# First batch of an attention and MLP kernel: sums of q and k by accumulating matmuls, sums of v and most lower parts of x on GpSimd

## The chip, the cores and the metric

The kernel runs on one core of a Trainium2 chip. The metric is the device time of one execution in microseconds. The engines are named as in the profile: PE (TensorE, with its weight loads as PEld), DVE (VectorE), ACT (ScalarE), POOL (GpSimd) and SP (SyncE, which here only issues DMAs).

## The reference

Attention with two branches, and an MLP on its result. q, k and v have the shape 8 x 8 x 576 x 64 (batch, heads, tokens, head size).

```python
q_d = q.reshape(B, H, Sd, 4, D).mean(axis=3)      # and k_d, v_d: means of four tokens
out_up = np.repeat(softmax(scale * q_d @ k_d.T) @ v_d, 4, axis=2)
mask = np.abs(pos[:, None] - pos[None, :]) < 4    # each token and three neighbours on either side
out_local = softmax(where(mask, scale * q @ k.T, -1e9)) @ v
x = (out_up + out_local).transpose(0, 2, 1, 3).reshape(4608, 512)
h = x @ w_in                                      # 512 x 2048
out = (np.maximum(h, 0) + alpha * np.minimum(h, 0)) @ w_out
```

w_in and w_out are 64-bit floats; everything else is fp32.

## The kernel before

**The MLP** is the long part. Its 4608 rows are cut into 18 chunks of 256 rows, and its 2048 hidden columns into 8 pairs of 128, which makes 144 steps. A step runs `hidden` (L761, PE: 24 matmuls), `slopes` (L772 to L776, ACT), `larger` (L782, POOL, in the first 12 steps, L784, DVE, later), `split` (L789, ACT and L71, POOL) and `product` (L818, PE: 12 matmuls). Each operand is held as two fp32r numbers, an upper part (the number rounded) and a lower part (what the rounding left), and three products of the parts make one product. x is held so in `xT[chunk]`, tiles xh and xl.

**The weights** arrive as 64-bit floats and are turned into fp32 by integer operations: `make` (L165) issues for each 1 MB block `magnitude` (L188, ACT), `reach` (L192, L193, DVE), `bits` (L197, L198, DVE), `upper` (L203 or L207, ACT) and `lower` (L211 or L215, DVE). The blocks are loaded into three slots in turn (`load_raw`, L134; L149 for w_in, L153 for w_out), so a load waits until `bits` has read the block three turns earlier. Five of the eight pairs are decoded ahead of the steps.

**Attention** of batches 1 to 7 is spread over the steps: `down` (L228) for the branch of means, `local` (L573) for the neighbours. `down` loads q, k and v of two heads in six loads into three buffers (L236) and folds four tokens into one on POOL (`fold`, L239; the adds appear as L74, the line of the helper `add`). Its `flip` (L254, PE) transposes the sums of q and k; as the tiles of these sums have one buffer each, the folds of the next pair of heads wait for it. The first pair of batch 1 comes before the steps.

**Attention of batch 0** is done first, by `first_batch`, whose generator `pair(hp)` handles heads 2hp and 2hp+1. Its loads are 72 partitions of 8 tokens: qk[hp] for q and k (L400), vt[hp] for v (L403), and windows of v (L412 to L416). PE transposes q and k (L432), ACT copies them out (L436, L440), and PE makes scores of 9 windows of 64 tokens against 70 keys (L448, L452). For the branch of means DVE adds in two halvings over q and over k (L460, in place, and L462), PE transposes the sums into the PSUM tile `fsum` (L467), ACT copies them out scaled (L470, L473) and PE makes the scores `sd` (L476). DVE adds over v likewise (L478, L480). Softmax runs on DVE and ACT (L330 to L338 for the means, L488 to L495 for the windows), PE transposes the probabilities (L344, L500) and multiplies by v (L508, L516), DVE joins the two branches (L519), ACT writes the upper part (L525) and DVE the lower part (L526). For w0 = 0 and 4 these are the chunks 0 and 1 of x; the last 64 tokens stay in `rest`. Pair 3 is the last of the four, and `hidden` of the first steps needs x of all four pairs.

**Order.** DVE, ACT, POOL and SP each run their instructions in one queue. Up to planned time 14 (in steps) that order is not written down: the framework orders the instructions of the program by a simulated timeline when it builds the kernel (`schedule_with_timeline_sim`), under the dependencies between tiles. Events from 14 on keep the order of their planned times. The batch-0 code, the decode of five pairs of weight blocks and the first 15 steps all lie in the first part. The DMAs of the start are issued by SP in the order of the string `ORDER` and then as their buffers are planned.

Of the kernel before, what the change touches and what calls it, by code (L numbers as in the profile page):

```python
# [9 lines left out]
F32 = mybir.dt.float32  # L10
# [3 lines left out]
ALU = mybir.AluOpType  # L14
# [4 lines left out]
FACTOR = 4  # L19
# [33 lines left out]
def tile_attention_moe(ctx: ExitStack, tc: tile.TileContext, q, k, v, w_in, w_out, alpha, out):  # L53
    nc = tc.nc
# [9 lines left out]
    def bank(kind, name):  # L64
        return ps_a.tile([128, 512], F32, tag=f"p{kind}", name=name, bufs=2 if kind == "d" else 1)

    def f32(ap):
        return ap.bitcast(F32)

    def sub(o, a, b):  # L70
        nc.gpsimd.tensor_tensor(o, a, b, op=ALU.subtract)  # L71

    def add(o, a, b):
        nc.gpsimd.tensor_tensor(o, a, b, op=ALU.add)  # L74
# [5 lines left out]
    ident = const.tile([128, 128], F32, name="ident")  # L80
# [274 lines left out]
    def operand(c):  # L355
        if c not in xT:
            pool = late if c % 3 == 2 else two
            xT[c] = [pool.tile([128, 4, T], F32R, tag=f"x{x}", name=f"x{x}{c}") for x in "hl"]
        return xT[c]
# [10 lines left out]
    def first_batch(st):  # L370
# [23 lines left out]
        qk, vt, vw = {}, {}, {}  # L394
# [24 lines left out]
        def pair_bank(kind, name):  # L419
            if kind == "o":  # L420
                return ps_o.tile([128, 512], F32, tag="po", name=name)
            if kind == "h":
                return ps_h.tile([128, 512], F32, tag="ph", name=name)
            return bank(kind, name)

        def pair(hp):
            halves = [slice(64 * e, 64 * e + 64) for e in range(2)]
            for x in range(2):
                for t0, nt in ((0, 4), (4, 4)):
                    ps = ps_h.tile([128, 512], F32, tag="ph", name=f"f{x}T{hp}{t0}")[:, 0:72 * nt]  # L430
# [12 lines left out]
            for part in ("sd", "ds")[EM[hp] == "b"]:  # L443
                if part == "s":
                    banks = []
                    for w0, nw in ((0, 7), (7, 2)):
                        ps = bank("q" if w0 == 0 else "l", f"fs{hp}{w0}")
                        nc.tensor.matmul(ps[:, 0:KEYS * nw], unit,  # L448
                                         wmask[:, w0:w0 + nw].rearrange("p w j -> p (w j)"), start=True, stop=False)
                        for i in range(nw):  # L450
                            w = w0 + i
                            nc.tensor.matmul(ps[:, KEYS * i:KEYS * i + KEYS], qb[:, w].rearrange("p e i -> p (e i)"),  # L452
                                             kT[:, WIN * w:WIN * w + KEYS], start=False, stop=(i == nw - 1))
                        banks.append((w0, w0 + nw, ps[:, 0:KEYS * nw].rearrange("p (w j) -> p w j", j=KEYS)))
                else:
                    sums = []
                    for i, x in enumerate("qk"):
                        lv = qk[hp][:, i].rearrange("p (g f) h d -> p g (f h d)", g=2)
                        s4 = lv[:, :, 0:256]
                        nc.vector.tensor_tensor(s4, lv[:, :, 0:256], lv[:, :, 256:512], op=ALU.add)  # L460
                        s2 = st.tile([72, 2, 128], F32, tag=f"fs2{x}", name=f"fs2{x}{hp}")
                        nc.vector.tensor_tensor(s2, s4[:, :, 0:128], s4[:, :, 128:256], op=ALU.add)  # L462
                        sums.append(s2)
                    ps = ps_h.tile([128, 512], F32, tag="ph", name=f"fsum{hp}")
                    for x in range(2):
                        for g in range(2):
                            nc.tensor.transpose(ps[:, (2 * x + g) * 72:(2 * x + g) * 72 + 72], sums[x][:, g],  # L467
                                                ident[:72, :72])
                    for e, r in enumerate(halves):
                        nc.scalar.mul(qd[r, :, 48 * e:48 * e + 48].rearrange("p b (i g) -> p b i g", g=2),  # L470
                                      ps[r, 0:144].rearrange("p (g b i) -> p b i g", g=2, b=3), DSCALE)
                    kd = st.tile([128, 144], F32, tag="fkh", name=f"fkd{hp}")
                    nc.scalar.copy(kd, ps[:, 144:288])  # L473
                    sd = bank("d", f"fsd{hp}")[:96, 0:432].rearrange("p (b c) -> p b c", b=3)
                    for bl in range(3):
                        nc.tensor.matmul(sd[:, bl, :], qd[:, bl, :], kd, start=True, stop=True)  # L476
            lv = vt[hp].rearrange("p h (g f) d -> p (h g) (f d)", g=2)
            nc.vector.tensor_tensor(lv[:, :, 0:128], lv[:, :, 0:128], lv[:, :, 128:256], op=ALU.add)  # L478
            vd = st.tile([72, 2, 2, 64], F32, tag="fs2v", name=f"fvd{hp}")
            nc.vector.tensor_tensor(vd.rearrange("p h g d -> p (h g) d"), lv[:, :, 0:64], lv[:, :, 64:128], op=ALU.add)  # L480
            if EM[hp] == "b":
                th = yield from down_probs(0, hp, sd)
            mx = one.tile([128, NWIN], F32, tag="lmx", name=f"fmx{hp}")
# [2 lines left out]
            p = st.tile([128, NWIN, KEYS], F32, tag="p", name=f"fp{hp}", bufs=2)  # L486
            for a_, b_, s in banks:
                nc.vector.tensor_reduce(out=mx[:, a_:b_], in_=s, axis=AX.X, op=ALU.max)  # L488
                nc.vector.tensor_tensor(p[:, a_:b_], s, mx[:, a_:b_].unsqueeze(2).to_broadcast([128, b_ - a_, KEYS]),
                                        op=ALU.subtract)  # L490
# [6 lines left out]
            for w0, nw in ((0, 4), (4, 4), (8, 1)):  # L497
                ps = pair_bank(FPT[hp][w0 // 4], f"fpt{hp}{w0}")
# [6 lines left out]
            for g in range(2):  # L505
                for e, r in enumerate(halves):
                    pr = th[g].rearrange("p (b e a) -> p b e a", b=3, e=2)[:, :, e]
                    nc.tensor.matmul(po[r, 0:144].rearrange("p (b a) -> p b a", b=3), vd[:, e, g], pr,  # L508
                                     start=(g == 0), stop=(g == 1))
            odf = st.tile([128, SD], F32, tag="odf", name=f"fod{hp}")  # L510
            nc.scalar.copy(odf, po[:, 0:144])
            for w0, nw in ((0, 4), (4, 4), (8, 1)):
                ps = pair_bank(FPV[hp][w0 // 4], f"fpv{hp}{w0}")
                for i in range(nw):
                    for e, r in enumerate(halves):
                        nc.tensor.matmul(ps[r, WIN * i:WIN * i + WIN], vw[hp][:, w0 + i, e, :],  # L516
                                         pT[:, w0 + i, 64 * e:64 * e + 64], start=True, stop=True)
                xs = rest[:, hp, :] if w0 == 8 else st.tile([128, 256], F32, tag="xs", name=f"fxs{hp}{w0}")
                nc.vector.tensor_tensor(  # L519
                    xs.rearrange("p (a r) -> p a r", r=4),  # L520
                    ps[:, 0:WIN * nw].rearrange("p (a r) -> p a r", r=4),
                    odf[:, 16 * w0:16 * (w0 + nw)].unsqueeze(2).to_broadcast([128, 16 * nw, 4]), op=ALU.add)
                if w0 < 8:
                    hi, lo = (t[:, hp, :] for t in operand(w0 // 4))
                    nc.scalar.copy(hi, xs)  # L525
                    nc.vector.tensor_tensor(lo, xs, f32(hi), op=ALU.subtract)  # L526
            yield

        return load_pair, load_windows, pair
# [322 lines left out]
    with tc.tile_pool(name="start", bufs=1) as start:  # L852
        load_pair, load_windows, pair = first_batch(start)
        todo = [(w, fp) for fp in range(NP) for w in range(2)]
        for step in ORDER.split():
            kind, i = step[0], int(step[1])
# [45 lines left out]
    for p in range(4 * (B - 1)):  # L902
        b, hp = 1 + p // 4, p % 4
# [92 lines left out]
```

## Time and profile before

| | |
|---|---|
| times of three runs | 998.66, 1002.87, 1002.91 us; median 1002.87 |
| span of the profiled execution | 999.3 us (its time around the span is not listed) |
| mean granted TensorE clock | 0.974 |
| busy, share of the span: PE | 954.3 us, 95% |
| DVE | 826.9 us, 83% |
| ACT | 558.1 us, 56% |
| POOL | 511.7 us, 51% |
| steady stream of `hidden` and `product` begins | 99.4 us |

A chain of work is followed back from the last instruction, at each step to what released it. In the timeline and in the groups of instructions, a name before the arrow is the tile written and the names behind it are those read; "x4" counts instructions that are put together in one row, and the bracket at the end gives the idle time of the engine before the row with what ended it.

### The profile page before, as it was taken

What the parts mean: (1) busy time and instruction counts of PE and PEld (TensorE: products, weight loads), DVE (VectorE), ACT (ScalarE), POOL (GpSimd) and SP (SyncE); (2) the same over time, 40 slices, a digit from 0 to 9 for tenths busy, and PEclk for the clock granted to TensorE, in tenths of its full rate; (3) what the DMA queues carried; (4) which work ended last, traced back from release to release, by engine and by line L of the source; (5) the groups of instructions that cost most, each with busy time, mean ns of one, the idle gap of its engine ahead of it and who ended that gap; (6) DMA issues with size and microseconds to landing.
All of it is one profiled execution on the core that took longest, in us unless ns stands there. A gap on an engine that the chain in (4) does not pass through costs nothing.

```text
span 999.3 us, 17971 instructions
## 1 busy us (share of the span) xinstructions
PE 954.3 (95%) x6402; PEld 851.0 (85%) x6402; DVE 826.9 (83%) x1336; ACT 558.1 (56%) x1483; POOL 511.7 (51%) x624
## 2 busy tenths in 40 slices
PE   5866999799999999999999999999999999999998
PEld 4745988698889988888988888898889888999897
DVE  6998888879898889988889888899898889997111
ACT  4856876355655564655565555565556564544442
POOL 2174867557576546655547355555456632324221
PEclk9956899899999999999999999999999999999999
DMA  8945723233423322332322423323333312210000
GB/s 193 231 162 181 253 88 101 71 107 92 128 86 91 121 71 90 115 100 77 121 73 88 123 86 83 115 85 87 114 91 113 98 55 68 80 33 22 1 22 22
DMA packets 63197, 98.28 MB, mean 98 GB/s; under 512 B 23556, under 2 KB 28932, under 8 KB 63108
## 3 DMA queue, kind: packets, MB, share of 16 engines
q1 hardware_dynamic: 62916, 96.88, 33.0%
q8 instruction: 50, 0.82, 0.4%
q10 hardware_dynamic: 192, 0.26, 0.1%
q14 instruction: 39, 0.32, 0.1%
HBM read 87.67 MB, written 9.44 MB: 97 GB/s over the span
## 4 chain that ended last, share of the span: by engine, by line
PE 87%; DVE 6%; DMA 3%; SPq 2%; ACT 1%; issue 1%; POOL 0%; ACTq 0%; DVEq 0%; POOLq 0%
PE h L761 40%; PE o L818 39%; PE s L267 2%; PE pv L301 2%; DMA raw<-in_moe_w_in 2%; PE xp L666 1%; PE pT L291 1%; SPq L400 1%; PE qkT L254 1%; DVE qk L598 1%; DMA raw<-in_moe_w_out 1%; DVE temp L197 1%; DMA ld<-in_k 0%; DVE temp L198 0%; DVE ls L602 0%
## 5 line engine op out<-in xcount | busy, mean ns | idle before, releaser
L71 POOL TENSOR_TENSOR gl<-t,gh 128x512 fp32r<-128x512 f32 x144 | 186.3, 1293 | 353.1 <-ACT gh L789 340.8
L772 ACT ACTIVATE t<-h,slope 128x256 f32<-128x256 f32 x288 | 136.5, 474 | 160.1 <-PE h L761 128.5
L761 PE MATMUL h<-xh,wih 128*128 128x256 f32 x1152 | 191.5, 287 | 13.3 <-ACT sh L774 6.9
L818 PE MATMUL o<-woh,gh 128*128 128x512 f32 x576 | 194.1, 408 | 0.0
L818 PE MATMUL o<-wol,gh 128*128 128x512 f32 x576 | 187.4, 396 | 0.0
L818 PE MATMUL o<-woh,gl 128*128 128x512 f32 x576 | 187.3, 396 | 0.0
L761 PEld LDWEIGHTS h<-xh,wih 128*128 128x128 f32 x1152 | 165.1, 191 | 24.4 <-ACT sh L774 7.1
L761 PE MATMUL h<-xh,wil 128*128 128x256 f32 x1152 | 185.7, 283 | 0.0
L761 PE MATMUL h<-xl,wih 128*128 128x256 f32 x1152 | 185.1, 282 | 0.0
L784 DVE TENSOR_TENSOR t<-h,t 128x512 f32<-128x512 f32 x132 | 90.6, 686 | 107.5 <-ACT h L776 105.8
L74 POOL TENSOR_TENSOR ld<-ld 72x256 f32<-72x256 f32 x168 | 136.1, 812 | 54.1 <-DMA ld<-in_q 48.8
L761 PEld LDWEIGHTS h<-xh,wil 128*128 128x128 f32 x1152 | 158.7, 191 | 0.4
L761 PEld LDWEIGHTS h<-xl,wih 128*128 128x128 f32 x1152 | 158.0, 190 | 0.5 <-POOL xl L71 0.2
L789 ACT CAST gh<-t 128x512 fp32r<-128x512 f32 x144 | 89.3, 620 | 121.1 <-DVE t L784 82.8
L602 DVE TENSOR_REDUCE ls<-qk 128x12 f32<-128x768 f32 (+1 forms) x126 | 136.2, 1083 | 2.9
L818 PEld LDWEIGHTS o<-woh,gl 128*128 128x128 f32 x576 | 108.1, 188 | 26.0
L818 PEld LDWEIGHTS o<-wol,gh 128*128 128x128 f32 x576 | 107.9, 188 | 24.7
L657 DVE TENSOR_TENSOR lb<-lb,pv 128x384 f32<-128x384 f32 x202 | 113.9, 564 | 5.6
L776 ACT ACTIVATE h<-h,sign 128x256 f32<-128x256 f32 x264 | 116.0, 439 | 0.0
L818 PEld LDWEIGHTS o<-woh,gh 128*128 128x128 f32 x576 | 99.2, 189 | 16.8 <-issue 3.0
L654 DVE TENSOR_TENSOR pv<-v,lb 128x1152 f32<-128x1152 f32 x84 | 93.6, 1115 | 2.6
L598 DVE TENSOR_TENSOR qk<-k,qp 128x768 f32<-128x768 f32 (+1 forms) x78 | 83.8, 1076 | 0.0
(151 smaller groups left out, 1136.7 us busy)
## 6 DMA issues: line engine op xcount, KB each, us to landing
k<-in_k SPq DMA_DIRECT2D x41, 384.0 KB
v<-in_v SPq DMA_DIRECT2D x41, 384.0 KB
out<-sg SPq DMA_DIRECT2D x140, 64.0 KB
raw<-in_moe_w_in SPq DMA_DIRECT2D x16, 512.0 KB
raw<-in_moe_w_out SPq DMA_DIRECT2D x16, 512.0 KB
ld<-in_q SPq DMA_DIRECT2D x56, 144.0 KB
ld<-in_k SPq DMA_DIRECT2D x56, 144.0 KB
ld<-in_v SPq DMA_DIRECT2D x56, 144.0 KB
```

The source lines that it names most:

```text
L71: nc.gpsimd.tensor_tensor(o, a, b, op=ALU.subtract)
L74: nc.gpsimd.tensor_tensor(o, a, b, op=ALU.add)
L598: nc.vector.tensor_tensor(st["pr"][:, :nd], window(tiles[u, "k"], half, d0, nd), st["qp", half].unsqueeze(1).to_broadcast([128, nd, 2, 192 ...
L602: nc.vector.tensor_reduce(out=st["s"][:, half, d0:d0 + nd, :].rearrange("p a b -> p (a b)"), in_=st["pr"][:, :nd].rearrange("p a h (t d) - ...
L654: nc.vector.tensor_tensor(st["pr"][:, :nd], window4(tiles[u, "v"], half, d0, nd), prob(half, d0, nd), op=ALU.mult)
L657: nc.vector.tensor_tensor(st["acc"], st["acc"], st["pr"][:, i], op=ALU.add)
L761: nc.tensor.matmul(ph[:, j], w[:, m, 128 * o:128 * o + 128], x[:, m, :], start=(i == 0), stop=(i == 11))
L772: nc.scalar.activation(t[:, j], hs[st][:, j], AF.Copy, scale=slope[:, f:f + 1])
L776: nc.scalar.activation(other[:, j], hs[st][:, j], AF.Copy, scale=sign[:, f:f + 1])
L784: nc.vector.tensor_tensor(gs[st], hs.pop(st), gs[st], op=ALU.max)
L789: nc.scalar.copy(gh, t)
L818: nc.tensor.matmul(outs[c][m], g[:, j, 128 * m:128 * m + 128], wo[w][n][:, o, :], start=(f == 0 and i == 0), stop=(f == NF - 1 and i == 2))
```

## The change

It touches only `pair` in `first_batch`, in three places.

1. The sums of four tokens of q and k no longer run on DVE. For each of the four parts of `fsum` PE issues four matmuls against the identity, one for each token, which accumulate in PSUM; so 16 matmuls per pair of heads take the place of four transposes, and the four DVE adds per pair (L460, L462) with their two tiles of sums are gone. qk[hp] is no longer overwritten.
2. The two sums of v per pair (L478, L480) move from DVE to POOL.
3. The lower part of x (L526) moves from DVE to POOL, but for the first chunk of pair 3.

```diff
-                    sums = []
-                    for i, x in enumerate("qk"):
-                        lv = qk[hp][:, i].rearrange("p (g f) h d -> p g (f h d)", g=2)
-                        s4 = lv[:, :, 0:256]
-                        nc.vector.tensor_tensor(s4, lv[:, :, 0:256], lv[:, :, 256:512], op=ALU.add)
-                        s2 = st.tile([72, 2, 128], F32, tag=f"fs2{x}", name=f"fs2{x}{hp}")
-                        nc.vector.tensor_tensor(s2, s4[:, :, 0:128], s4[:, :, 128:256], op=ALU.add)
-                        sums.append(s2)
                     ps = ps_h.tile([128, 512], F32, tag="ph", name=f"fsum{hp}")
                     for x in range(2):
                         for g in range(2):
-                            nc.tensor.transpose(ps[:, (2 * x + g) * 72:(2 * x + g) * 72 + 72], sums[x][:, g],
-                                                ident[:72, :72])
+                            for f in range(FACTOR):
+                                nc.tensor.matmul(ps[:, (2 * x + g) * 72:(2 * x + g) * 72 + 72],
+                                                 qk[hp][:, x, FACTOR * g + f].rearrange("p h d -> p (h d)"),
+                                                 ident[:72, :72], start=(f == 0), stop=(f == FACTOR - 1))
...
-            nc.vector.tensor_tensor(lv[:, :, 0:128], lv[:, :, 0:128], lv[:, :, 128:256], op=ALU.add)
+            add(lv[:, :, 0:128], lv[:, :, 0:128], lv[:, :, 128:256])
             vd = st.tile([72, 2, 2, 64], F32, tag="fs2v", name=f"fvd{hp}")
-            nc.vector.tensor_tensor(vd.rearrange("p h g d -> p (h g) d"), lv[:, :, 0:64], lv[:, :, 64:128], op=ALU.add)
+            add(vd.rearrange("p h g d -> p (h g) d"), lv[:, :, 0:64], lv[:, :, 64:128])
...
-                    nc.vector.tensor_tensor(lo, xs, f32(hi), op=ALU.subtract)
+                    if hp == 3 and w0 == 0:
+                        nc.vector.tensor_tensor(lo, xs, f32(hi), op=ALU.subtract)
+                    else:
+                        sub(lo, xs, f32(hi))
```

`add` and `sub` are the helpers of L73 and L70, which issue the operation on POOL.

## The prediction

> **What bounds the kernel now.** I read the chain that ended last first, then asked for busy times by stage, with the stages cut where the chain changes its engine.
>
> ```profile
> 0.00:44.70 44.70, 30.39 (x215) 26.49 (x215) 34.36 (x74) 26.65 (x68) 5.64 (x26) 1.00 0.96 212
> 44.70:73.80 29.10, 18.08 (x155) 13.42 (x156) 29.10 (x49) 18.79 (x48) 23.50 (x15) 0.66 0.54 176
> 73.80:99.40 25.60, 16.39 (x118) 13.71 (x118) 22.28 (x32) 16.47 (x42) 11.37 (x10) 0.63 0.54 171
> 99.40:180.00 80.60, 80.60 (x528) 72.46 (x529) 71.79 (x104) 57.52 (x149) 59.44 (x68) 0.96 0.44 141
> ...
> 196.40:999.30 802.90, 798.24 (x5324) 716.35 (x5324) 653.79 (x1061) 431.69 (x1162) 404.20 (x497) 1.00 0.28 83
> ```
>
> The columns are the stage, its length, the busy time of PE, PEld, DVE, ACT and POOL with their instructions, the granted clock, the DMA share and GB/s. Up to 44.7 us the DMA engines are 96% busy and bound the stage. From 44.7 to 73.8 us DVE is busy for all 29.10 us: it is the bound there, and POOL beside it is 81% busy. From 99.4 us PE is busy without a gap, and after 196.4 us for 798.24 of 802.90 us. A change to the first batch can therefore act on little but how early PE's steady stream starts.
>
> The chain of work says the same in order of time (start, length, what):
>
> ```profile
> 40.50 4.19 DMA raw<-in_moe_w_in
> 44.69 0.17 DVE fp L489
> ...
> 73.76 1.93 PE fpt L500 x8
> ...
> 81.36 0.54 POOL s2q L74
> ...
> 92.20 3.92 DMA raw<-in_moe_w_in
> ...
> 99.37 5.49 PE h L761 x24
> ```
>
> DMA holds the chain until 44.69, DVE until pair 3's probabilities are normalised (L495, 73.7). Then PE transposes them, runs on to the flip of batch 1's first pair, POOL folds the next pair behind it, SP gets to the next weight load only behind the loads into the folded buffers, ACT takes that weight ahead of the activations of `slopes`, and then `hidden` goes on.
>
> **The change part by part.** *Taken from DVE in the DVE-bound stretch.* The shares of the chain between 44.7 and 73.8 by line, and the removed pieces that this line does not list:
>
> ```profile
> by line: DVE temp L197 17.4%; DVE temp L198 12.5%; DVE wil L211 7.6%; DVE xl L526 6.7%; DVE temp L193 6.3%; DVE temp L192 6.2%; DVE wol L215 5.2%; DVE fp L495 5.0%; DVE fsm L492 5.0%; DVE fqk L460 3.9%; DVE dnb L330 3.5%; DVE fxs L519 3.4%;
> ...
> 46.45 0.34 DVE fs2q L462
> ...
> 49.67 0.87 DVE fs2k L462
> ...
> 51.26 0.10 DVE fvd L480
> ...
> 68.50 0.32 DVE fvd L480
> ```
>
> Of 29.1 us, xl's 6.7% are 1.95 and fqk's 3.9% are 1.14. With 0.34 + 0.87 + 0.10 + 0.32 that makes 1.95 + 1.14 + 1.63 = **4.7 us** of a chain that stays on DVE throughout. What is late next in this stretch is again DVE (mostly the decode of the weights, L192 to L215), so I count the removal in full. Its ends are 0, if that decode then waits for weights, and 4.7.
>
> *Taken from DVE before 44.7.* Between 20 and 44.7 us DVE's instructions on the tiles fqk (L460, L462) and fv (L478, L480) are, in this order:
>
> ```profile
> 20.00:44.70 24.70, 5.00 (x9) 1.00 1.03 228
> ...
> 20.00:44.70 24.70, 1.78 (x3) 1.00 1.03 228
> ```
>
> That is 6.8 us. The DMA share of 1.03 hides most of it: weights that have not arrived cannot be decoded earlier. At worst it is worth 0, at best 6.8 plus the wait for v below. I value it by the lag of one operation that had its input:
>
> ```profile
> 34.22 0.74 ACT L491 ACTIVATE fp<-fp 128x630 f32<-128x630 f32 x1
> ...
> 35.24 0.69 DVE L478 TENSOR_TENSOR fv<-fv 72x512 f32<-72x512 f32 x1 [2.03 <-DMA fv<-in_v]
> ...
> 36.91 0.80 DVE L492 TENSOR_REDUCE fsm<-fp 128x9 f32<-128x630 f32 x1
> ```
>
> Pair 1's exponentials end at 34.96, and their sum starts 1.95 us later, because DVE stood 2.03 us at the head of its queue for v's data and then ran sums that now go away. The wait moves to POOL. I take **2.0 us**, with 0 and 6.8 + 2.0 = 8.8 as ends; it is the lower part, since DMA is the bound of that stage.
>
> *Added to POOL.* Eight additions for v and seven subtractions. These are the nearest rows, and what happens when both engines work at once:
>
> ```profile
> L71 POOL TENSOR_TENSOR gl<-t,gh 128x512 fp32r<-128x512 f32 x144 | 186.3, 1293 | 353.1 <-ACT gh L789 340.8
> ...
> 46.39 3.87 POOL L74 TENSOR_TENSOR ld<-ld 72x256 f32<-72x256 f32 x2 [39.82 <-DMA ld<-in_q]
> ...
> 51.09 2.83 POOL L74 TENSOR_TENSOR ld<-ld 72x256 f32<-72x256 f32 x1
> ...
> 65.47 0.72 POOL L74 TENSOR_TENSOR ld<-ld 72x256 f32<-72x256 f32 x1
> ...
> 40.66 0.41 DVE L526 TENSOR_TENSOR xl<-fxs,xh 128x256 fp32r<-128x256 f32 x1
> ...
> 64.53 0.67 DVE L526 TENSOR_TENSOR xl<-fxs,xh 128x256 fp32r<-128x256 f32 x1
> ```
>
> A subtraction of 128x256 has half of gl's elements, so an estimate of 0.65 us; beside a busy DVE it can take up to four times that, as the same fold took 0.72 and 2.83 us. The first sum of v has 72x512 outputs, twice the fold, so 1.4 us, and the second 0.7: 8.5 us in all for four pairs. POOL is idle for 39.82 us up to 46.39, which covers the v sums; what is queued behind them are batch 1's folds, whose data come only then. Without that cover they would push those folds back by as much. The four subtractions that DVE makes between 44.9 and 73.8 come to 2.6 to 10 us of POOL, just before a time in which POOL waits:
>
> ```profile
> POOL s2q L74 <- PE qkT L254: 9.8, 1, 9.8
> ...
> SPq L236 <- POOL s2k L74: 10.7, 4, 4.9
> ```
>
> So those folds end later, but inside the 9.8 us for all but the upper end. The price that I do count is on DVE: an operation beside POOL's took 0.67 instead of 0.41 us, 0.26 more, and four times that is **1.0 us**. The ends are 0 (POOL's work falls beside other reads) and four times 0.54, 2.2 us, by the sum of q or k:
>
> ```profile
> 35.85 0.68 DVE L460 TENSOR_TENSOR fqk<-fqk 72x512 f32<-72x512 f32 x1
> ...
> 46.70 1.22 DVE L460 TENSOR_TENSOR fqk<-fqk 72x512 f32<-72x512 f32 x1
> ```
>
> The Trainium skill, SBUF — State Buffer, section "SBUF: two separate sides", speaks against this part: VectorE, in instructions with two SBUF inputs among others, and GpSimd take a shared port pair as an exclusive lock for a whole instruction, and whichever comes second blocks fully. By that rule a subtraction on GpSimd could hold VectorE up for longer than the subtraction it is rid of, and the four would lose about 1 us (4 x 0.65 against 4 x 0.41) where the sum here gains 0.9 by them (1.95 less 1.0). The trace agrees that such pairs slow each other (0.67 against 0.41), not that all of it is lost.
>
> *Added to PE.* Per pair 16 accumulating matmuls take the place of 4 transposes, 48 more in all. Matmuls of about the same number of columns:
>
> ```profile
> 26.27 4.11 PE L452 MATMUL fs<-kT,qb 128*128 128x70 f32 x18 [0.90 <-ACT kT L440]
> ...
> 50.37 2.12 PE L452 MATMUL fs<-kT,qb 128*128 128x70 f32 x18
> ```
>
> That is 0.23 us each early and 0.12 later: 6 to 11 us of PE between 12 and 53 us. I cost this at nothing: PE is busy for only 30.39 of the first 44.7 us, where DMA is the bound, and the sums no longer wait for two DVE operations. If that cover is gone, pair 3's group costs 12 x 0.12 = 1.4 us; the lower end is a gain of the two DVE operations, already in the first term.
>
> *After 73.8.* Pair 3's first lower part stays on DVE; the other subtractions there lie beside the chain. I take the tail from 73.76 to 99.37 as it is, moved as a whole.
>
> Sum: 4.7 + 2.0 - 1.0 = **5.7 us** earlier. The profiled span of 999.3 us becomes 993.6. The profiled execution's time around its span is not listed; the span lies between the lowest run (998.66) and the median (1002.87), so I take the same step from the median: **997.2 us**.
>
> **The rivals.** (A) *The whole backlog moves.* If pairs 1 and 2 get ahead while the weights still arrive, the upper end of the second term holds: 4.7 + 8.8 - 1.0 = 12.5, about **990 us**. For it: DVE's queue is what held pair 1's sum. Against it: DVE already idles for 10.3 of the first 44.7 us, waiting for inputs, and removed work adds to that.
>
> (B) *Another engine keeps the start; the change moves work and not the end.* The chain's second half runs through POOL, SP, a DMA and ACT. If POOL's folds, longer by up to 10 us against 9.8 of idle time, keep SP from the weight loads, DVE is faster and then waits for its next weight. Of the 5.7 us some 0 to 3 are left: **1001 us**. For it: SP stood 10.7 us for s2k already, and DVE's 29.10 of 29.10 is not the last wait of the start.
>
> (C) *Slower: POOL's queue.* POOL works in order. If pair 3's second subtraction stands in its queue ahead of the folds that start at 81.36, POOL waits for an upper part that ACT ends at 89.69:
>
> ```profile
> 89.30 0.39 ACT L525 CAST xh<-fxs 128x256 fp32r<-128x256 f32 x1
> ```
>
> That is 8.3 us later, and about 1.5 for a subtraction beside DVE, less the 5.7 gained: 4.1 us slower, **1007 us**. It decides as soon as that wait is longer than the 5.7 us gained. Against it: those folds are released 8 us before the subtraction's input is there, so a queue in order of readiness has them first.
>
> **How the numbers follow.** The forecast (992 to 1000) has a chance of 0.50, A 0.13, B 0.25, C 0.12. A measurement of this kernel can tell about 0.5%, 5 us, from no change: below 997.9 and above 1007.9. The forecast gives 0.37 faster and 0.13 same; A 0.13 faster; B 0.03 faster and 0.22 same; C 0.03 same and 0.09 slower. That is faster 0.53, same 0.38, slower 0.09. The range 988 to 1005 takes in the forecast, most of A and B, with the ends of the unknown costs between them, and leaves out most of C and A's far end.
>
> **What would show it.** Right: in the DVE-bound stretch L460, L462, L480 and L526 are gone and nothing fills their place; pair 3's L495 ends near 68 instead of 73.7; PE's unbroken `hidden` stream starts near 93.7 instead of 99.4. Wrong: DVE idle for weights between 45 and 90 (B); a POOL subtraction that waits for ACT with folds behind it (C); DVE operations far above their durations here, which would make the 1.0 us for contention too small; or pair 3's scores late because of PE's sums.

## The result and the profile after

The changed kernel takes 1012.61 us (median of four runs, 1011.23 to 1013.83), the kernel before 1000.79 us (median of four). The ratio is 1.0117, with a 95% interval of [1.0082, 1.0151]: **slower by 1.2%**, where 997.2 us and a gain were forecast, and outside the range (988 to 1005). The profiled execution has a span of 1009.4 us, 10.1 more than before. In the ratios below slow executions, such as one of the kernel before at 1179.87 us, are left out, while the medians are over all executions.

Busy time by stage of the kernel after, cut at the same times as in the prediction (columns: stage, length, busy time of PE, PEld, DVE, ACT and POOL with their instructions, granted clock, DMA share, GB/s):

```profile
0.00:44.70 44.70, 33.45 (x187) 31.96 (x189) 22.43 (x40) 20.30 (x45) 13.58 (x32) 1.00 0.95 222
44.70:73.80 29.10, 24.71 (x149) 22.03 (x145) 27.28 (x37) 17.22 (x38) 20.03 (x19) 0.96 0.56 197
73.80:99.40 25.60, 23.05 (x151) 21.26 (x149) 21.46 (x35) 16.11 (x38) 3.86 (x4) 0.50 0.35 125
99.40:180.00 80.60, 75.22 (x518) 67.72 (x518) 61.67 (x101) 57.93 (x156) 51.57 (x62) 0.90 0.41 132
196.40:1009.40 813.00, 808.39 (x5410) 724.75 (x5408) 663.81 (x1075) 439.15 (x1182) 412.31 (x506) 1.00 0.27 83
```

DVE did lose work: 22.43 us up to 44.7 where it had 34.36, and it is no longer full in the second stage. PE has gained it: 3.1, 6.6 and 6.7 us more than before in the first three stages, together 16.4, and in the third, where PE had been idle for more than a third, it is now 90% busy. In this trace the relief of DVE brought nothing forward, because PE became the late one. The chain of work after, between 73 and 104 us (start, length, what):

```profile
74.45 1.04 ACT wih L203
76.25 0.74 PE f1T L432 x4
...
80.53 6.31 PE fsum L460 x30
...
90.80 1.67 PE fs L452 x8
...
102.73 0.72 DVE fp L489
103.60 2.11 PE fpt L494 x9
```

In this stretch the chain of before ran first through PE and ACT, then through POOL, SP and two DMAs; it now runs mostly through PE, and its longest piece is pair 3's group of sums. Pair 3's last window scores (L452) end at 92.5 us, behind that group: ACT had copied out their input by 80.4 us (kT, L440), and they started at 86.6. Its probabilities (L489; L495 before) are normalised at 103.5 us instead of 73.7. That is 30 us, and yet the span grew by 10: part of the delay is caught up later, where the kernel before waits.

### The profile page after: what moved, and what is told of

It is laid out like the page before. It is cut to its first block, busy times and chain, and to the rows that moved or that the text cites. A ratio compares the mean times of both kernels' runs of the same rounds, so it can differ in the third digit from the quotient of the medians.

```text
span 1009.4 us, 18177 instructions
## 1 busy us (share of the span) xinstructions
PE 981.2 (97%) x6514; PEld 882.3 (87%) x6514; DVE 811.7 (80%) x1305; ACT 559.5 (55%) x1483; POOL 514.7 (51%) x639
## 4 chain that ended last, share of the span: by engine, by line
PE 90%; SPq 3%; DVE 2%; DMA 2%; POOL 1%; issue 1%; ACT 1%; DVEq 0%; ACTq 0%; POOLq 0%
PE o L815 40%; PE h L758 40%; PE s L267 2%; SPq L400 2%; PE pv L301 2%; PE xp L663 1%; PE pT L291 1%; DMA ld<-in_q 1%; PE qkT L254 1%; PE fsum L460 1%; PE fpv L510 1%; POOL ld L74 1%; DVE temp L198 0%; DMA raw<-in_moe_w_in 0%; PE fpt L494 0%
## 5 line engine op out<-in xcount | busy, mean ns | idle before, releaser
L758 PEld LDWEIGHTS h<-xh,wil 128*128 128x128 f32 x1152 | 156.6, 189 | 0.1
L74 POOL TENSOR_TENSOR ld<-ld 72x256 f32<-72x256 f32 x168 | 128.3, 767 | 14.1 <-DMA ld<-in_q 10.6
```

The source lines that it names most:

```text
L758: nc.tensor.matmul(ph[:, j], w[:, m, 128 * o:128 * o + 128], x[:, m, :], start=(i == 0), stop=(i == 11))
```

## The experiments

Each ratio is against runs of the kernel before that were taken beside it, whose medians were 999.96 (e1 to e4), 999.69 (e5 to e8), 1001.22 (e9 to e11), 999.7 (e12 to e15) and 1000.45 us (e16 to e18). The parts of the change are called 1 (sums of q and k on PE), 2 (sums of v on GpSimd) and 3 (lower parts on GpSimd).

### Each side of the change, and PE's matmuls by themselves

e1 is part 1 alone, e2 is parts 2 and 3 alone. e3 is the whole change with one matmul instead of four for each part of fsum; e4 is the kernel before with matmuls added that nothing reads.

```diff
 e3 (from the kernel after)
-                            for f in range(FACTOR):
+                            for f in range(1):
...
-                                                 ident[:72, :72], start=(f == 0), stop=(f == FACTOR - 1))
+                                                 ident[:72, :72], start=True, stop=True)
 e4 (from the kernel before, behind each transpose of the sums)
+                            for f in range(FACTOR):
+                                nc.tensor.matmul(ps[:, 288 + 72 * g:360 + 72 * g],
+                                                 sums[x][:, g], ident[:72, :72],
+                                                 start=(f == 0), stop=(f == FACTOR - 1))
```

> The kernel before with the first part of the change alone: the sums of q and k by accumulating matmuls; v's sums and x's lower parts stay on DVE. In the changed kernel these matmuls are 128 instructions in the trace, 32 per pair in 6.5 to 7.1 us of PE. Theory 1 (the length of these matmuls in PE's queue makes the change slow): about the changed kernel's time, 1008 to 1016 us. Theory 2 (the work moved to GpSimd makes it slow): at or below the kernel before, 994 to 1001 us.

> The changed kernel without its first part: q and k are summed by DVE as before; v's sums and seven of the eight lower parts run on GpSimd. Theory 1 (PE's matmuls): at or below the kernel before, 994 to 1002 us; by the prediction's own terms (xl and v's sums off DVE, less 1 us of contention) about 2 us faster. Theory 2 (GpSimd): 1008 to 1016 us.

> The changed kernel with one matmul instead of four for each part of fsum: the sums of q and k take only the first of each four tokens. DVE is as free as in the changed kernel and GpSimd has the same work; only three quarters of the matmuls are gone (8 instructions per pair instead of 32). Theory 1: 990 to 1000 us, which is what the prediction expected of the whole change. Theory 2: 1008 to 1016 us. Theory 3 (any other order of the start costs about this much, whatever is in it): above 1005 us.

> The kernel before with 16 matmuls against the identity added per pair, which accumulate in columns of fsum that nobody reads; DVE's sums and the transposes stay. DVE and GpSimd have exactly the work they had before. Theory 1: the 32 instructions per pair cost as they do in the changed kernel, without its relief of DVE: 1010 to 1020 us. Theory 2: 998 to 1003 us, as PE had free time there.

| run | median, us | ratio to before, 95% |
|---|---|---|
| e1, part 1 | 1002.70 | 1.0024 [1.0001, 1.0047] |
| e2, parts 2 and 3 | 1009.11 | 1.0094 [1.0078, 1.0109] |
| e3, whole change, one matmul for four | 1000.84 | 0.9998 [0.9982, 1.0015] |
| e4, before with 16 more matmuls per pair | 1011.18 | 1.0122 [1.0099, 1.0144] |

Neither theory holds alone: e1 lies between the two forecasts, e2 is as slow as theory 2 has it, and e4 as theory 1 has it. But the pieces add up. e4 prices PE's matmuls at 1.22% (12 us); the way from e3 to the whole change, which adds three quarters of them, gives 1.19%. What DVE's relief from the sums of q and k is worth is the step from e4 to e1, 0.98%, and from e2 to e3, 0.96%: some 9.7 us, more than all that was forecast for the relief. (These steps also change PE's work a little: the transposes of the sums go, and e3 has one matmul for each.) Part 1 is therefore a gain and a loss of nearly the same size. And the two parts on GpSimd, which were to gain, cost 0.94% (e2; 0.93% from e1 to the whole change).

How much PE work the sums are, in the timeline of PE after (one group of sums for each pair; 30 or 32 matmuls in a row of the view, the rest of each group in another):

```profile
12.04 7.05 PE L460 MATMUL fsum<-ident,fqk 72*128 72x72 f32 x32
...
29.68 6.67 PE L460 MATMUL fsum<-ident,fqk 72*128 72x72 f32 x30 [1.34 <-ACT kT L440]
...
53.65 6.67 PE L460 MATMUL fsum<-ident,fqk 72*128 72x72 f32 x30 [0.73 <-ACT kT L440]
...
80.32 6.51 PE L460 MATMUL fsum<-ident,fqk 72*128 72x72 f32 x30
```

and in that of before, pair 3's transposes:

```profile
47.50 0.34 PE L467 MATMUL fsum<-ident,fs2q 72*128 72x72 f32 x2
...
52.33 0.29 PE L467 MATMUL fsum<-ident,fs2k 72*128 72x72 f32 x2
```

The program issues 16 matmuls for a pair, and the trace has 32: an fp32 matmul is two instructions, a transpose one. At 0.22 us each a pair's sums take 7 us where pair 3's transposes took 0.6.

### GpSimd's parts, one at a time

e5 is e2 with both lower parts of pair 3 left on DVE, e6 is part 2 alone, e7 part 3 alone. e8 is another way to relieve DVE: four reductions per pair from the PSUM tiles of the transposes of q and k, in place of the four additions, the transposes of the sums and a copy.

```diff
 e5 (from e2)
-                    if hp == 3 and w0 == 0:
+                    if hp == 3:
 e8 (from the kernel before; the adds, L467 and L473 go)
+                    nc.vector.tensor_reduce(out=sqk[:, 72 * (2 * x + t0 // 4):72 * (2 * x + t0 // 4) + 72],
+                                            in_=ps.rearrange("p (t a) -> p a t", t=nt), axis=AX.X, op=ALU.add)
```

> e2 (v's sums and the lower parts on GpSimd, q and k summed by DVE) with both lower parts of pair 3 on DVE instead of the first alone. In e2, in e3 and in the changed kernel the last lower part stands in GpSimd's queue behind the folds of the next pair (in e2 at 102.3 us), and ACT's slopes start right after it, because their tile takes over memory that it reads. If that wait is what GpSimd's part costs (theory 2a), this gives 999 to 1004 us against e2's 1009.1. If the cost is the contention of the two engines or the wait behind folds earlier (theory 2b), 1006 to 1010 us.

> The kernel before with v's two sums per pair on GpSimd and nothing else. Theory 2b in the form that the v sums stand ahead of batch 1's folds in GpSimd's queue and the weight loads behind them: 1004 to 1010 us. Theory 2a, or the lower parts as the only cost: 997 to 1001 us.

> The kernel before with seven of eight lower parts on GpSimd and nothing else. If the lower parts carry GpSimd's cost: 1005 to 1010 us; if v's sums carry it: 997 to 1002 us. By the sums of e1, e2 and e4 so far (matmuls on PE +12, q and k off DVE -9.5, GpSimd's two parts +9.5), e6 and e7 together should lose about 9.5 us.

> The kernel before with the sums of q and k taken by DVE from the PSUM tiles of the transposes (one reduction of 288 to 72 columns for each four tokens) in place of the four adds, the four transposes of fsum and the copy of kd. Theory 1 says that q's and k's sums off DVE gain about 9.5 us when PE does not pay for them. Here DVE is relieved by an estimate of 4 x (2.5 - 4 x 0.43) = 3 us and PE and ACT of the transposes and a copy: 995 to 999 us. If only the complete removal from DVE counts, or the reductions hold the transposes' buffers: 999 to 1004 us.

| run | median, us | ratio to before, 95% |
|---|---|---|
| e5 | 1008.66 | 1.0079 [1.0049, 1.0110] |
| e6, part 2 | 1006.09 | 1.0058 [1.0036, 1.0079] |
| e7, part 3 | 1005.58 | 1.0050 [1.0030, 1.0071] |
| e8 | 1004.47 | 1.0045 [1.0029, 1.0060] |

Parts 2 and 3 each cost about half of e2's loss, and pair 3's last subtraction is not where it lies (e5 against e2: no difference that can be told). e8 is no cheaper way: it is slower than both of its forecasts. The trace of e7 offered a cause, in the timeline of DVE:

```profile
59.20 1.06 DVE L495 TENSOR_TENSOR fp<-fp,frs 128x630 f32<-128x630 f32 x1
67.37 0.42 DVE L519 TENSOR_TENSOR fxs<-fpv,fod 128x256 f32<-128x256 f32 x1 [7.11 <-POOL xl L71]
```

The bracket says that DVE stood idle for 7.11 us in the middle of the stretch that it had bounded, because GpSimd's subtraction still had to read the only buffer of xs. It looked like the answer; e12 tests it below.

### The order of the program

The framework chooses the order of the instructions by a simulated timeline, so every edit also moves others. EM says for each pair whether the means ("b") or the window scores ("a") come first.

```diff
 e9 (before) and e10 (after); e11 (after) has 'bbbb'
-EM = 'bbba'
+EM = 'aaaa'
```

> The kernel before with one string changed, so that every pair makes its window scores ahead of the sums of q and k instead of pair 3 alone (the same operations; the planner gives PE and DVE another order). Theory 3 (the order that the planner makes of the start matters as much as the work): away from the kernel before by 4 us or more, most likely slower. Theories 1 and 2 (the work that was moved decides): 997 to 1003 us.

> The changed kernel with the same string changed: PE now has the window scores of each pair in its queue ahead of the 32 instructions that sum q and k. Theory 1 as the cause of the loss through what waits behind these instructions: 1003 to 1008 us. If only PE's total counts: 1010 to 1014 us. Theory 3: anywhere from 1000 to 1018.

> The changed kernel with pair 3 in the order of the other pairs: sums of q and k and the softmax of the means ahead of the windows. Theory 1 through what waits behind: 1010 to 1016 us, as pair 3's window scores stay behind the sums. Theory 3: away from the changed kernel's 1012.6 by 4 us or more on either side.

Before with scores first takes 997.62 us, 0.9974 [0.9952, 0.9997]; after takes 1016.72 us, 1.0164 [1.0139, 1.0188], with scores first and 1015.21 us, 1.0140 [1.0107, 1.0173], with means first. So e9 lies inside the forecast of theories 1 and 2, but close to its lower end, and e10 missed theory 1's (1003 to 1008 us): it is some 5 us slower than after. Its trace shows why this says nothing on theory 1. The planner did not put the scores ahead of the sums; pair 3's group still stands in front of them:

```profile
77.79 7.03 PE L460 MATMUL fsum<-ident,fqk 72*128 72x72 f32 x32
84.76 0.48 PE L510 MATMUL fpv<-fpT,vw 70*64 70x64 f32 x4
85.17 2.84 PE L452 MATMUL fs<-kT,qb 128*128 128x70 f32 x12
```

The sums on PE with the scores ahead of them were therefore not tried. Order alone moves the time by some 2 to 5 us, down in e9 and up in e10 and e11; no order tried makes up for the 12. A single effect of 5 us, such as those of e6 and e7, is no larger than what an order can do. The 12 us of the matmuls and the 9.7 of the relief are larger, and both come out of two pairs of runs. e9 does the same operations as the kernel before and is the fastest version found, ahead of both kernels, by little.

### The single buffers

```diff
 e12 (e7), e14 (after), e15 (before)
-... st.tile([128, 256], F32, tag="xs", name=f"fxs{hp}{w0}")
+... st.tile([128, 256], F32, tag="xs", name=f"fxs{hp}{w0}", bufs=2)
 e13 (e6), e14 (after), e15 (before)
-            vd = st.tile([72, 2, 2, 64], F32, tag="fs2v", name=f"fvd{hp}")
+            vd = st.tile([72, 2, 2, 64], F32, tag="fs2v", name=f"fvd{hp}", bufs=2)
```

> Part 3 alone (the lower parts by GpSimd, 1005.6 us, +5.0) with two buffers for the tile xs in place of one; nothing else is edited, but the planner sets a somewhat different order. Theory A, the single buffer: in the run with part 3 alone the vector engine's next fxs addition waited 7.6, 2.0 and 7.1 us for GpSimd's subtraction, which still reads xs; with two buffers these waits go below 1 us each and the time falls by 4 to 6 us, to 999-1002 (0.998 to 1.002 of before). Theory B, GpSimd is slow and late by itself (0.72 to 4.25 us where the vector engine took less, behind folds that wait for their loads): the waits go, the time stays at 1004-1007. C, something else: a time above 1008.

> Part 2 alone (v's sums by GpSimd, 1006.1 us, +5.8) with two buffers for the tile fvd in place of one; TensorE, VectorE and ScalarE keep their order row by row, on GpSimd the second additions of pairs 1, 2 and 3 move ahead. Theory A, the single buffer: the second addition of a pair stands in GpSimd's queue until the fdv matmuls of the pair before have read fvd (2.5 us twice with part 2 alone, 3.9 and 10.7 us with the whole change), with the second batch's folds behind it; with two buffers that wait goes and the time falls to 999-1002. Theory B, the additions themselves take GpSimd's time and the shared port from the vector engine: 1004-1007 again, with the waits gone from GpSimd's rows.

> The whole change with two buffers for xs and for fvd. If the two single buffers are what GpSimd's parts cost (theory A, +9.3 to 9.9 us of the change's 11.8), the matmuls remain (+11.5) and the vector engine's relief (-9.5): 1001-1004, 1.000 to 1.004 of before. Theory B, GpSimd's parts cost that by their own time and place: 1009-1014 as the whole change.

> The control: the kernel before with two buffers for xs and for fvd. The vector engine does both the reading and the writing of xs in its own order, so a second buffer removes no wait that the profile of before shows; theory A and B both give 998-1003. A fall by over 3 us would mean that the second buffer, or the order that the planner then sets, is worth something without GpSimd, and would have to be taken off what the other two show.

| run | median, us | ratio to before, 95% | without the second buffer |
|---|---|---|---|
| e12 | 1007.28 | 1.0078 [1.0058, 1.0098] | 1.0050 (e7) |
| e13 | 1007.63 | 1.0081 [1.0062, 1.0100] | 1.0058 (e6) |
| e14 | 1011.89 | 1.0122 [1.0101, 1.0142] | 1.0117 (after) |
| e15 | 1002.38 | 1.0019 [1.0003, 1.0036] | 1 (before) |

Theory A falls in e12, e13 and e14; e12 and e13 even lie a little above theory B's forecast. The waits for xs are gone from e12, where DVE waits for only two things between 40 and 100 us:

```profile
DVE temp L192 <- ACT temp L188: 4.8, 1, 4.8
DVE fqk L460 <- PE f1T L432: 0.3, 1, 0.3
```

and the time is no better. A wait of 7 us on the busiest engine of the stage was worth nothing. What is left is a wait for a weight to unpack (temp), and that one leads on.

### Where the loss is: the restart at 196 us

In the kernel before, PE waits once more at the second batch's operand, which DVE's attention writes (xf, L678) and ACT rounds (xh, L692). The row of that restart in before, then in e9, e6, e2, e4 and e14:

```profile
196.33 1.22 PE L761 MATMUL h<-xh,wih 128*128 128x256 f32 x4 [3.98 <-ACT xh L692]
```

```profile
193.30 1.15 PE L761 MATMUL h<-xh,wih 128*128 128x256 f32 x4 [2.69 <-ACT xh L692]
```

```profile
201.26 1.22 PE L761 MATMUL h<-xh,wih 128*128 128x256 f32 x4 [4.85 <-ACT xh L692]
```

```profile
205.25 1.23 PE L764 MATMUL h<-xh,wih 128*128 128x256 f32 x4 [3.99 <-ACT xh L695]
```

```profile
206.10 1.22 PE L765 MATMUL h<-xh,wih 128*128 128x256 f32 x4 [2.69 <-ACT xh L696]
```

```profile
206.47 0.74 PE L758 MATMUL h<-xh,wih 128*128 128x256 f32 x4 [2.69 <-ACT xh L689]
```

From there to the end PE has next to no idle time, in every kernel. So the span less the restart is nearly the same number (each row is one profiled execution; single executions of the kernel before range from 997 to 1006 us):

| run | restart, us | span, us | difference |
|---|---|---|---|
| e9 | 193.30 | 995.6 | 802.3 |
| e3 | 195.22 | 999.2 | 804.0 |
| e15 | 195.76 | 998.0 | 802.2 |
| before | 196.33 | 999.3 | 803.0 |
| e1 (no wait there) | 200.27 | 1001.2 | 800.9 |
| e8 | 200.59 | 1003.6 | 803.0 |
| e7 | 201.04 | 1004.5 | 803.5 |
| e6 | 201.26 | 1003.6 | 802.3 |
| e5 | 201.36 | 1004.1 | 802.7 |
| e12 | 202.25 | 1005.6 | 803.4 |
| e13 | 202.34 | 1004.8 | 802.5 |
| e2 | 205.25 | 1007.3 | 802.1 |
| e4 | 206.10 | 1008.2 | 802.1 |
| e14 | 206.47 | 1008.1 | 801.6 |
| e11 (no wait there) | 208.18 | 1009.0 | 800.8 |
| after (no wait there) | 208.67 | 1009.4 | 800.7 |
| e10 | 211.06 | 1014.1 | 803.0 |

The first steps of the MLP, which the prediction took for the thing to hasten, do not decide: their first matmul with a weight's lower part starts at 85.8 us in before and at 113.0 in after, 27 us apart, and of that 12.3 are left at the restart. The kernel before waits 6.9 us up to 99.4 and 4.0 us up to the restart; after 122 us the kernel after waits 0.7 us in all up to the restart:

```profile
PE o L815 <- ACT gh L786: 0.7, 1, 0.7
```

So a kernel can be held at this point in two ways: PE gets there late (after, e1, e11), or the operand does (before and all others). The two are not far apart. In e4 only PE got more work, and the operand came 10 us later than in before, so PE's sums, with the order that the planner sets for them, delay the operand too; and e10 and e14, versions of the whole change, wait 2.8 and 2.7 us for it.

### What makes the operand late with GpSimd's parts

From 96.9 to 152 us DVE of before does almost nothing but unpack weights, and only then comes the attention that writes the operand. The loads of these weights (raw, L149) stand in SyncE's in-order queue among the loads of the second batch (ld, L236), which wait for buffers that GpSimd's folds free. That queue in before:

```profile
82.78 1.70 SPq L236 DMA_DIRECT2D ld<-in_v  x2
91.79 0.30 SPq L236 DMA_DIRECT2D ld<-in_q  x1
92.20 0.91 SPq L149 DMA_DIRECT2D raw<-in_moe_w_in  x2
...
95.32 2.05 SPq L149 DMA_DIRECT2D raw<-in_moe_w_in  x4
```

and in e6, where the second of two such loads goes out 8.5 us behind the first and the weights right behind it:

```profile
88.86 8.86 SPq L236 DMA_DIRECT2D ld<-in_q  x2
97.82 2.78 SPq L149 DMA_DIRECT2D raw<-in_moe_w_in  x5
```

What those weights do to DVE, in before and in e6 (the first row of their unpacking):

```profile
96.85 0.70 DVE L192 TENSOR_SCALAR temp<-temp 128x512 f32<-128x512 f32 x1 [2.28 <-ACT temp L188]
```

```profile
102.43 0.70 DVE L192 TENSOR_SCALAR temp<-temp 128x512 f32<-128x512 f32 x1 [6.05 <-ACT temp L188]
```

5.6 us late here, 4.9 us late at the restart; that the one makes the other is so far only argued. e16 to e18 take the second batch's loads, but for its first pair, off SyncE's queue:

```diff
 e16 (from e6), e17 (from e2), e18 (from before)
-            nc.sync.dma_start(st[i].rearrange("p g f d -> p (g f d)"),
+            (nc.gpsimd if b == 1 and hp else nc.sync).dma_start(st[i].rearrange("p g f d -> p (g f d)"),
```

> Part 2 alone (v's sums by GpSimd: 1006.1 us, span 1003.6), and the loads of the second batch's q, k and v for pairs 1 to 3 issued from GpSimd's queue in place of SyncE's. In ten runs the span is 802.0 to 803.5 us longer than the moment at which TensorE starts again on the second batch's operand (196.3 us before, 201.3 with part 2 alone): what is lost is lost before that. Theory D: there SyncE's in-order queue stood 8.1 us at such a load, which waited for GpSimd's fold, and the weights' loads behind it went out at 97.8 us (before: 92.2 and 95.3); the vector engine's unpacking of these weights, and all that stands behind it, started 5.6 us late. With the loads off that queue the weights go out by 93 us, TensorE starts again by 197 and the median is 999-1002. Theory E, the weights wait for their own memory or for the unpacking before them, not for the queue: they go out at 96 us or later, 1004-1007.

> Parts 2 and 3 (1009.1 us, span 1007.3, TensorE starts again at 205.3), with the same loads issued from GpSimd's queue. There the weights went out at 99.1 and 103.0 us. Theory D: by 95 us, a start at 199 or before and 1001-1004. Theory E (the weights wait for memory that GpSimd's last subtraction, at 102.3 us, still holds, or for the vector engine's earlier unpacking): the queue is free and they go out at 98 us or later, 1006-1010.

> The control: the kernel before with the same loads on GpSimd's queue. SyncE's queue waited 7.2 us in all at such loads there too, the weights went out at 92.2 and 95.3 us. Theory D: they go out 0 to 3 us earlier, 996-1001; if it falls as far as the other two, the queue is a cost of every version and not what GpSimd's parts added. Theory E: no change, 998-1003. In all three the span should again be some 802 to 803.5 us longer than the moment of the restart.

| run | median, us | ratio to before, 95% | restart, us | span, us |
|---|---|---|---|---|
| e16 | 1003.58 | 1.0035 [1.0019, 1.0050] | 199.77 | 1003.4 |
| e17 | 1006.23 | 1.0062 [1.0039, 1.0084] | 200.20 | 1003.3 |
| e18 | 1003.03 | 1.0032 [1.0013, 1.0051] | 197.07 | 1000.3 |

Spans less restarts are 803.1 to 803.6: the relation holds. Neither theory holds as it was written. The weights of e16 went out at 94.18 us, between the two bounds, and its time lies between the two forecasts; those of e17 began to go out at 92.37 us, as theory D has it, and its time is that of theory E. The control is slower than theory D has it: the move has a price of its own, 0.32%. Where that comes from was not tested; GpSimd issues these loads at about 0.53 us apiece. Nor does the moment at which the weights go out set the restart alone: in e18 they began to go out at 87.77 us and their unpacking started 2.7 us earlier than in before (94.19 against 96.85), and the restart came 0.7 us later. Against that control, part 2 costs 0.03% instead of 0.58%, and parts 2 and 3 cost 0.30% instead of 0.94%. The two differences, 0.55% and 0.64%, are each uncertain by about 0.33% (the half-widths of their three intervals, squared, added and rooted), so by the medians most of the cost of GpSimd's parts goes away with the shared queue. The profiled restarts give less for part 2: e16 restarts 2.7 us behind e18, where e6 was 4.9 us behind before; e17 3.1 us behind, where e2 was 8.9. So the queue carries a good part of the cost, and how much is open; this also takes it that the move costs e16 and e17 what it costs e18. In e16 a rest can be seen on DVE: SyncE waits there for the unpacking of earlier weights, whose last operation (L198) ends at 94.11 us, in e18 at 87.70. In e17 there is also a rest of the other theory. SyncE's waits there between 70 and 125 us:

```profile
SPq L153 <- DVE temp L198: 24.1, 5, 6.9
SPq L149 <- DVE temp L198: 11.7, 2, 6.4
SPq L149 <- POOL xl L71: 7.5, 1, 7.5
```

The weight loads of pairs 6 and 7 stand for 7.5 us behind a subtraction on GpSimd, in memory that the first batch used before them, and most of the rest is for the unpacking of earlier weights.

## Why the prediction was wrong, step by step

**What bounds the kernel** was read half right. DVE's queue did hold the stretch from 44.7 to 73.8 us. The stages that it lists jump from 180.0 to 196.4 us, though, and PE is busy for only 10.58 of the 16.4 us between: there lies the wait at the restart, so that an earlier steady stream alone need not end the kernel earlier. And "PE is busy for only 30.39 of the first 44.7 us, where DMA is the bound" was taken as room for more work, and it is not room: what stands behind a group of sums in PE's order waits for it, as pair 3's scores did from 80.4 to 86.6 us.

**"Added to PE ... I cost this at nothing"** is the step that failed. The estimate of 6 to 11 us counted 48 matmuls at the time of one row entry, though the row quoted for it shows 18 for nine windows; the trace has 128 instructions for the sums, about 28 us in four groups of 7. And they were not hidden: added alone they cost 12 us (e4), three quarters of them taken out of the change give 11.8 back (e3). The prediction's price without cover, 1.4 us for pair 3's group, turned out as 6.5 us for that group alone: 28 more instructions where 12 were counted, at 0.22 us instead of 0.12. That some 25 us of added work come to 12 at the end fits the later waits of before, shown above.

**"Taken from DVE", 4.7 and 2.0 us.** For q and k the direction was right and the size too small: of the two terms 2.35 us and part of 2.0 were theirs, and the relief measured 9.7. For v and the lower parts it was wrong in sign: 2.37 us of the 4.7 were theirs, and moving them cost 5.8 and 5.0 us (e6, e7), 9.4 together.

**"Added to POOL"** said that the folds end later "but inside the 9.8 us". Its sizes were about right: in after the first sums of v take 1.26 to 1.80 us, and in e7 a subtraction takes 0.72 to 4.25. (Its 8.5 us for the sums of v is 8.4 by its own terms.) But the idle time up to 46.39 us does not cover the v sums: in after the second sums of pairs 1 to 3 run at 46.6, 68.5 and 95.4 us, the last two behind waits of 3.9 and 10.7 us for PE's fdv. And it priced GpSimd's work and not who waits for the folds: SyncE's queue, then DVE's unpacking. The words for this are in rival B (GpSimd's folds "keep SP from the weight loads"); its mechanism is the one that e16 to e18 bear out in part for these two parts, but it was given a time of 1001 us, as if it could only eat up the gain. The 1.0 us for contention was not measured by itself and stays open, and so does the rule of the Trainium skill quoted there.

**The tail "as it is, moved as a whole"** was wrong: it is not moved as a whole. The start of the steady stream moved by some 20 us, the restart by 12.3.

**The rivals.** C had the sign, but not the mechanism: in the kernel after, the folds that it speaks of wait for PE's flip, not for a subtraction:

```profile
110.10 0.86 POOL L74 TENSOR_TENSOR s2q<-ld 72x128 f32<-72x128 f32 x2 [8.46 <-PE qkT L254]
```

No rival had PE as the engine that becomes late, though the last sentence of the prediction names "pair 3's scores late because of PE's sums", which is what the trace shows.

**What stays open.** It is open what the matmuls would cost with the scores ahead of them in PE's order. It is open, too, why GpSimd's parts cost the whole change as much (0.93%) as they cost the kernel before (0.94%), though after does not wait for the operand (e10 and e14 do). In one place after can be seen to lose time. Pair 2's window scores are done at 65.7 us, but DVE unpacks weights first, and takes their maximum (fmx) at 70.5:

```profile
65.17 1.21 DVE L211 TENSOR_TENSOR wil<-temp,wih 128x1024 fp32r<-128x1024 f32 x1
66.30 1.21 DVE L197 SCALAR_TENSOR_TENSOR temp<-raw,temp 128x1024 int32<-128x1024 int32 x1
67.62 0.69 DVE L192 TENSOR_SCALAR temp<-temp 128x1024 f32<-128x1024 f32 x1
68.23 1.22 DVE L198 SCALAR_TENSOR_TENSOR temp<-raw,temp 128x1024 int32<-128x1024 int32 x1
69.36 1.22 DVE L193 TENSOR_SCALAR temp<-temp 128x1024 int32<-128x1024 int32 x1
70.50 0.87 DVE L482 TENSOR_REDUCE fmx<-fs 128x7 f32<-128x490 f32 x2
```

ACT's exponential waits for that, and a cast of weights behind it for DVE's next unpacking. ACT's copies of pair 3's q (qb) stand behind both, and PE waits 2.23 us for them:

```profile
76.25 0.74 PE L432 MATMUL f1T<-ident,fqk 72*128 72x72 f32 x4 [2.23 <-ACT qb L436]
```

In e1 the same maximum was taken 0.3 us after its scores. So it looks like an order that the framework chose once DVE had less to do; that was not tried by itself.

## What to carry to other kernels

An idle share of an in-order engine is not room: before giving it work, find what stands behind that work in its queue and who waits for it, and count instructions in the trace, not calls in the program. When an engine is relieved, ask for the later point where the kernel really waits (here the second batch's operand, needed at 196 us in before and 801 to 804 us ahead of the end in every version) and follow what releases it, through the DMA queue too. A long wait in a profile is a suspect and not a verdict: one of 7 us on the busiest engine of its stage went away here, and nothing was gained.

## What was unexpected in the hardware

The sums, small fp32 matmuls, ran at one pace whatever granted clock the profile gives. They took 0.22 us an instruction in the rows above at 12, 30 and 54 us, and so they did at 80 us; the profile of after gives these granted clocks (last three columns: clock, DMA share, GB/s):

```profile
12.00:19.00 7.00, 7.00 (x35) 7.00 (x35) 1.84 (x2) 1.42 (x2) 4.71 (x3) 1.00 1.03 231
...
53.60:60.40 6.80, 6.75 (x32) 6.75 (x33) 6.80 (x10) 3.78 (x8) 6.42 (x6) 1.00 0.57 197
...
80.30:86.90 6.60, 6.60 (x34) 6.60 (x32) 6.60 (x9) 3.55 (x9) 2.16 (x2) 0.50 0.00 0
```

So the granted clock of 1.00 did not mean full speed there: the window scores, 18 matmuls of 70 columns, took 2.12 us in before at 50 us and 4.11 us at 26 us (both in the prediction), with a granted clock of 1.00 in both stretches. In after, 14 of them took the longer time per instruction, again at a granted clock of 1.00 (61.4 to 65.7 us):

```profile
61.46 3.19 PE L452 MATMUL fs<-kT,qb 128*128 128x70 f32 x14
```

The Trainium skill, TensorE: Matmul & The Clock Gate, section "Part 1: The HAM clock gate (the "warmup" mystery)", says that the clock doubles after about 3.4 us of sustained activity. These rows do not agree: 32 matmuls one behind the other for 7.05 us did not get faster, nor did the window scores behind the third group, in the row above. Behind the restart in before the pace does change, after some 4.4 us: four matmuls of `hidden` take 1.05 us up to there and 0.64 us afterwards, as in these two rows:

```profile
199.91 1.05 PE L761 MATMUL h<-xh,wil 128*128 128x256 f32 x4
...
204.89 0.64 PE L761 MATMUL h<-xh,wih 128*128 128x256 f32 x4
```

What sets the pace of the first batch's matmuls stays open, and with it whether sums at half this time would have paid.
